# Clustered attention with two feed-forward layers: an order planned around VectorE and GpSimd, and weight pieces split on ScalarE

## Chip, cores and metric

One NeuronCore of one Trainium2 chip. The metric is the device time of one execution in microseconds (us), median of three runs. Engine names: PE is TensorE, DVE is VectorE, ACT is ScalarE, POOL is GpSimd, SP is SyncE, which issues the DMAs.

## What is computed

Two batches of eight heads, 768 positions, head size 64. A query sees only the keys that fall to the same one of 16 centroids; then come two feed-forward layers (512 to 2048 to 512), the first with SiLU, the second with PReLU:

```python
mask = q_assign[:, :, :, None] == k_assign[:, :, None, :]
scores = scale * np.matmul(q, k.transpose(0, 1, 3, 2))
scores = np.where(mask, scores, -1000000000.0)
scores = scores - np.max(scores, axis=-1, keepdims=True)
attn = np.exp(scores)
attn = attn / (np.sum(attn, axis=-1, keepdims=True) + 1e-09)
out = np.matmul(attn, v)                   # (2, 8, 768, 64) -> x: (1536, 512)
h = x @ w_in;   x = (h * (1.0 / (1.0 + np.exp(-h)))) @ w_out        # layer 1
h = x @ w2_in;  y = (np.maximum(h, 0.0) + alpha * np.minimum(h, 0.0)) @ w2_out   # layer 2
```

The inputs are float64 in HBM, so each weight matrix is 8 MB there.

## The kernel before

**Numbers.** Every matrix product is made of three fp16 products: each operand is a high half plus a low half, and high*high, high*low and low*high are added in PSUM.

**Attention.** 96 units: 12 tiles of 128 queries times 8 heads. `front` makes the scores of a unit on PE (lines 692 and 696), DVE scales them in PSUM and takes their minimum (L706), ACT makes the exponential (L711) and its high half (L718), DVE the low half (L720: fp32 value and fp16 high half in, both in SBUF). A transposing DMA (L726) turns both halves, and `back` multiplies them by V on PE (L738). K, V and Q are scaled and split first (`prep_k_*`, `prep_v*`, `prep_q_*`), largely on ACT and POOL; `pow2_scale` turns a sum of squares into a scale with a DVE step (L345) and two tiny ones, mostly on POOL (L350, L353).

**Weights.** Each of the four matrices comes in 8 pieces of 1 MB (`load_piece`, L792). `to_f32` makes fp32 of the float64 bits: two ACT operations (L803, L807) and two DVE operations with two SBUF inputs each (L814, L817). `sum_sq` takes the piece's sum of squares on PE and DVE (L848, L850), and `split` makes the fp16 halves, each 128x1024. What it costs where depends on a letter of `SPLIT`: "d" makes the high half on POOL (L824) and the low half on DVE (L825, two SBUF inputs); "a" makes the high half on ACT (L829) and the low half on DVE (L830); "b" is two ACT operations (L834, L835) and the low half on POOL (L836); "c" is POOL, ACT, POOL (L838 to L840). Before, the 32 letters hold 20 d, 8 b, 4 c and no a. Pieces of an "in" matrix are split one by one, and their raw buffer then takes the next load; pieces of an "out" matrix share one scale and are split when all eight are summed (`late`).

**Layers.** Layer 1 runs in 7 chunks of queries between the attention units: first product L1077, SiLU (L1084, L1085, L1088, L1089), second product L1108. The second layer's weights are prepared when attention is done, since they use its memory. Layer 2 has three stretches of 512 queries: `split_x2` (L1165, L1166), first product L1179 with 16 blocks, PReLU on DVE (L1188 and L1189 read PSUM), high half on ACT (L1192), low half on DVE (L1193, two SBUF inputs), then the second product L1210. Three PSUM banks take the blocks in turn.

**Order.** `Plan` takes all instructions in the order in which they were written, gives each a cost from a small table (`costs`), and places them engine by engine: each engine takes the earliest-written instruction that is ready in planned time (`run`). The result is fixed as the order in each engine's queue; waits are on data alone, and no wait is added for the plan's times.

Of the kernel before, what the change touches and what calls it, by code (L numbers as in the profile page):

```python
# [34 lines left out]

K_SCALE_ON = ("aaaa", "pppa")
V_SCALE_ON = ("papa", "appp")
SPLIT = ("dddddddd", "dddbdddb", "dbdbdbdb", "dccdcbbc")
EXP_ON = ("aaaaaaaa", "aaaaaaaa", "aaaaaaaa", "aaaaaaaa")
P_LO_DVE = range(96)  # L40

# [4 lines left out]
class Plan:  # L46
# [4 lines left out]
    def __init__(self, instructions):  # L51
        self.ins = [
            i for i in instructions
            if self.engine(i) in self.ENGINES and type(i).__name__ not in ("BassTilePoolBoundary", "InstRegisterMove")
        ]
        self.eng = [self.ENGINES.index(self.engine(i)) for i in self.ins]
        self.cost = [self.costs(i) for i in self.ins]
        self.deps = [[] for _ in self.ins]
        self.order_only = [[] for _ in self.ins]
        self.data_deps()  # L60
# [12 lines left out]
    def costs(self, i):  # L73
# [21 lines left out]
        rate = 400.0 if run >= 4096 else 290.0 if run >= 2048 else 380.0  # L95
        return (0.47, 1.3, n * 512 / 1000.0 / rate)

    def cells(self, a):
        import numpy as np

        b = a.bass_ap
        name = b.tensor.name.rsplit("_", 1)[0]
        if type(b.tensor).__name__.startswith("DRam"):
            return None, None
        it = 2 if a.dtype in (F16, BF16) else 4
        dims = [list(x) for x in a.ap]
        at = np.array([b.offset % dims[0][0]], dtype=np.int64)
        for st, c in dims[1:]:
            if st:
                at = (at[:, None] + np.arange(c) * st).ravel()  # L110
        cell = np.unique(at * it // 4)
        if name[0] in "sxmw" and (name[1:].isdigit() or len(name) == 1):
            return "ps" + name, np.unique(cell // 512)
        return name, cell

# [35 lines left out]
    def run(self, prio):  # L151
        import heapq

        N, ne = len(self.ins), len(self.ENGINES)
        after = [[] for _ in range(N)]
        left = [0] * N
        for n in range(N):
            for d in self.deps[n]:
                after[d].append((n, False))
            for d in self.order_only[n]:  # L160
                after[d].append((n, True))
            left[n] = len(self.deps[n]) + len(self.order_only[n])
        ready = [0.0] * N
        free, busy = [0.0] * ne, [-1.0] * ne
        now, later = [[] for _ in range(ne)], [[] for _ in range(ne)]
        order = [[] for _ in range(ne)]
        queue = end = 0.0
        for n in range(N):
            if not left[n]:
                heapq.heappush(later[self.eng[n]], (0.0, prio[n], n))  # L170
        for _ in range(N):
            while True:
                best = None
                for e in range(ne):
                    while later[e] and later[e][0][0] <= free[e]:
                        t, p, n = heapq.heappop(later[e])
                        heapq.heappush(now[e], (p, n))
                    t = free[e] if now[e] else later[e][0][0] if later[e] else None
                    if t is not None and (best is None or t < best[0]):
                        best = (t, e)  # L180
                t, e = best
                if now[e]:
                    break
                free[e] = t
            n = heapq.heappop(now[e])[1]
            s, c = free[e], self.cost[n]
            kind = self.ENGINES[e]
            if kind == "PE":
                if s > busy[e] + 0.02:
                    s += 0.06  # L190
                free[e] = busy[e] = s + c[0]
                done = s + c[0] + 0.23
                own = free[e]
            elif kind == "SP":
                b = max(s + c[1], queue)
                queue = b + c[2]
                free[e] = max(s + c[0] + 0.06, queue - 7.5 + c[0])
                done = own = queue + 0.33
            else:
                free[e] = s + max(c[0] - 0.075, 0.04)  # L200
                done, own = s + c[0] + 0.06, s + c[0]
            end = max(end, done)
            order[e].append(n)
            for m, only in after[n]:
                at = s if only else own if self.eng[m] == e else done
                ready[m] = max(ready[m], at)
                left[m] -= 1
                if not left[m]:
                    heapq.heappush(later[self.eng[m]], (ready[m], prio[m], m))
        return end, order  # L210
# [19 lines left out]
def cluster_attention_silu_prelu(  # L230
# [729 lines left out]
    def attention():  # L960
# [348 lines left out]
```

## Time and profile before

| what | us |
|---|---|
| median of three runs (lowest, highest) | 863.17 (862.83, 863.89) |
| profiled execution, its own time | 861.21 |
| span of its instructions | 859.3 |
| PE busy, share of the span | 726.8 (85%) |
| DVE busy | 558.5 (65%) |
| ACT busy | 437.9 (51%) |
| POOL busy | 216.8 (25%) |

The profiled execution's own time is 1.9 us over its span and 1.96 us under the median. Shares over the whole span mix stages with different limits, so the profile is read by stage. PE's clock is given as a granted share: 1.00 is its upper level of 2.4 GHz, half of it the lower level of 1.2 GHz, and a value in between is a stretch with both.

### The profile page before, as it was taken

To read this page: it belongs to the slowest core of one execution; us is meant where nothing else is said; L and a number is where in the kernel's file an instruction comes from. 1 tells how busy PE (TensorE), PEld (TensorE's weight loads), DVE (VectorE), ACT (ScalarE), POOL (GpSimd) and SP (SyncE) were. 2 spreads that over 40 slices of the span, in tenths; PEclk is the share of its full clock that TensorE was granted. 3 is DMA by queue.
4 is the path that set the end of the run, shared out by engine and by line. 5 is a ranking of instruction groups with operands and counts; after the bars stand their busy time and mean duration, and the time that the engine had idled before them with its cause. 6 is when DMAs were issued, how large, how long until landed. Compare 5 with 4: busy or idle time off the path is not lost.

```text
span 859.3 us, 16824 instructions
## 1 busy us (share of the span) xinstructions
PE 726.8 (85%) x6932; PEld 508.5 (59%) x6932; DVE 558.5 (65%) x1012; ACT 437.9 (51%) x713; POOL 216.8 (25%) x273
## 2 busy tenths in 40 slices
PE   2455557868888799999899979989989998999998
PEld 2334346657776687788777868777434443444443
DVE  5588897897868776837976876777780068106710
ACT  7835675746667756736766775865241023102210
POOL 4752412482424632200221045108200000000000
PEclk9999557789999899999999979999999999999999
DMA  9977898759999698935897984530000000000000
GB/s 281 258 189 186 184 308 138 124 104 181 139 184 163 133 175 145 153 61 100 145 146 124 280 189 154 197 147 1 1 1 19 31 1 1 12 25 13 1 24 25
DMA packets 241596, 101.89 MB, mean 119 GB/s; under 512 B 217328, under 2 KB 227568, under 8 KB 241392
## 3 DMA queue, kind: packets, MB, share of 16 engines
q1 hardware_dynamic: 241520, 100.83, 54.7%
q8 instruction: 54, 0.88, 0.4%
q14 instruction: 22, 0.18, 0.1%
HBM read 44.08 MB, written 3.15 MB: 55 GB/s over the span
## 4 chain that ended last, share of the span: by engine, by line
PE 24%; issue 16%; DVE 5%; DMA 5%; ACT 2%; POOL 2%; POOLq 0%; SPq 0%; ACTq 0%; DVEq 0%
PE w L1210 6%; PE w L1179 4%; PE w L1108 4%; PE m L1210 4%; DMA arena<-arena 2%; PE m L1179 2%; DMA arena<-in_moe_w_out_dram 2%; PE x L738 1%; DVE arena L1193 1%; DVE arena L1188 1%; PE w L1077 1%; DMA arena<-in_moe_w_in_dram 1%; DVE arena L1189 1%; PE m L1108 1%; ACT arena L1192 1%
## 5 line engine op out<-in xcount | busy, mean ns | idle before, releaser
L1108 PE MATMUL w<-arena 128*128 128x256 f16 (+1 forms) x1248 | 133.8, 260 | 9.5 <-DVE arena L825 6.4
L1108 PEld LDWEIGHTS <-arena 128*128 128x128 f16 x1344 | 117.2, 100 | 26.6 <-DVE arena L825 7.1
L1077 PE MATMUL w<-arena 128*128 128x256 f16 (+1 forms) x1200 | 130.3, 260 | 2.8 <-DVE arena L1085 2.4
L1077 PEld LDWEIGHTS <-arena 128*128 128x128 f16 x1344 | 116.8, 100 | 18.2 <-issue 4.1
L711 ACT ACTIVATE arena<-s,stat 128x768 f32<-128x768 f32 x96 | 86.1, 897 | 71.7 <-DVE s L706 39.5
L720 DVE TENSOR_TENSOR arena<-arena 128x768 f16<-128x768 f32 x96 | 99.4, 1038 | 32.0 <-ACT arena L718 31.8
L706 DVE TENSOR_SCALAR_CACHE_REDUCE s<-s,stat 128x768 f32<-128x768 f32 x96 | 97.7, 1021 | 31.8 <-PE s L696 30.1
L1179 PEld LDWEIGHTS <-arena 128*128 128x128 f16 x576 | 57.1, 99 | 76.5 <-issue 11.9
L718 ACT ACTIVATE arena<-arena 128x768 f16<-128x768 f32 x96 | 80.0, 840 | 34.2 <-DMA arena<-arena 33.8
L1210 PEld LDWEIGHTS <-arena 128*128 128x128 f16 x576 | 56.3, 98 | 68.0
L738 PE MATMUL x<-arena 128*128 128x64 f16 x1728 | 74.8, 202 | 22.7 <-DMA arena<-arena 22.1
L350 POOL TENSOR_SCALAR stat<-stat 128x1 int32<-128x1 int32 x49 | 17.7, 360 | 296.8 <-DVE stat L345 215.9
L1179 PE MATMUL w<-arena 128*128 128x512 f16 x384 | 88.0, 384 | 2.6 <-DVE arena L1189 2.5
L738 PEld LDWEIGHTS <-arena 128*128 128x128 f16 x1728 | 68.2, 104 | 33.3 <-DMA arena<-arena 29.8
L1210 PE MATMUL w<-arena 128*128 128x512 f16 x384 | 83.7, 379 | 0.0
L1192 ACT ACTIVATE arena<-arena,stat 128x512 f16<-128x512 f32 x48 | 34.5, 722 | 94.3 <-DVE arena L1189 94.3
L692 PE MATMUL s<-arena 80*128 80x384 f16 x192 | 69.0, 359 | 10.1 <-ACT arena L711 10.0
L1188 DVE TENSOR_SCALAR arena<-w,stat 128x512 f32<-128x512 f32 x32 | 23.9, 745 | 82.0 <-PE w L1179 82.0
L696 PE MATMUL s<-arena 128*128 128x384 f16 x192 | 69.5, 362 | 0.0
L1193 DVE SCALAR_TENSOR_TENSOR arena<-arena,stat 128x512 f16<-128x512 f32 x48 | 38.5, 805 | 29.5 <-ACT arena L1192 29.5
L814 DVE SCALAR_TENSOR_TENSOR arena<-arena 128x1024 int32<-128x1024 int32 x32 | 39.6, 1237 | 15.5 <-ACT arena L807 15.5
L1179 PE MATMUL m<-arena 128*128 128x512 f16 x192 | 45.4, 387 | 3.1 <-DVE arena L1189 3.0
(155 smaller groups left out, 1071.5 us busy)
## 6 DMA issues: line engine op xcount, KB each, us to landing
arena<-in_moe_w_in_dram SPq DMA_DIRECT2D x16, 1024.0 KB, 6.2
arena<-in_moe_w_out_dram SPq DMA_DIRECT2D x16, 1024.0 KB, 5.3
arena<-in_k_dram SPq DMA_DIRECT2D x8, 384.0 KB, 4.6
arena<-in_q_dram SPq DMA_DIRECT2D x6, 512.0 KB, 4.8
arena<-in_v_dram SPq DMA_DIRECT2D x8, 384.0 KB, 5.7
out_dram<-arena SPq DMA_DIRECT2D x12, 256.0 KB, 2.0
arena<-arena SPq DMA_TRANSPOSE x149, 4.1
arena<-in_moe_alpha_dram SPq DMA_DIRECT2D x1, 1024.0 KB, 5.4
```

Of the source, the lines that this page charges most:

```text
L692: nc.tensor.matmul(out=sc[:, j, :hs], lhsT=qt2[0:D + C, h], rhs=kt2[0:D + C, h % 2, j * hs:(j + 1) * hs], start=True, stop=False,)
L696: nc.tensor.matmul(out=sc[:, j, :hs], lhsT=qt1[:, h], rhs=kt1[:, h % 2, j * hs:(j + 1) * hs], start=False, stop=True,)
L706: nc.vector.tensor_scalar(sc[:, :, :hs], sc[:, :, :hs], nd_cols[:, H * (n % 2) + h:H * (n % 2) + h + 1], None, op0=ALU.mult, op1=ALU.min, ...
L711: nc.scalar.activation(out=view(o, F32, 2, hs), in_=sc[:, :, :hs], func=ACTF.Exp, scale=-1.0, bias=bias, accum_out=sums[n % 2][:, h:h + 1],)
L718: nc.scalar.activation(out=hl[:, 0], in_=p, func=ACTF.Copy)
L720: en.tensor_tensor(out=hl[:, 1], in0=p, in1=hl[:, 0], op=ALU.subtract)
L738: nc.tensor.matmul(out=x_ps[0][:, h], lhsT=pt[:, ph * T + t], rhs=vt[:, h % 2, t, vh], start=(i == 0), stop=(i == 3 * T - 1),)
L1077: nc.tensor.matmul(out=hp[:, ff], lhsT=wi[:, a, kd, ff * 128:ff * 128 + 128], rhs=mov(bb, kd), start=(i == 0), stop=(i == 3 * KD - 1),)
L1108: nc.tensor.matmul(out=acc, lhsT=wo[:, a, f % 2, dt * 128:(dt + 1) * 128], rhs=g[:, f, bb], start=(i == 0), stop=(i == 3 * KF - 1),)
L1179: nc.tensor.matmul(out=hp, lhsT=in_piece(o_a + 24 * KB, f // 2)[:, a, kd, f % 2 * 128:][:, :128], rhs=x[bb][:, kd], start=(i == 0), stop=( ...
L1193: nc.vector.scalar_tensor_tensor(out=g[:, f, 1], in0=gf, scalar=l2[:, 0:1], in1=g[:, f, 0], op0=ALU.mult, op1=ALU.subtract,)
L1210: nc.tensor.matmul(out=acc, lhsT=g[:, f, a, t * 128:(t + 1) * 128], rhs=out_piece(o_w, f // 2)[:, bb, f % 2], start=(i == 0), stop=(i == 3 ...
```

## The change

Two things. **The planner** knows a shared resource of DVE and POOL: `takes_port` is true for every POOL operation but a memset, and for DVE's tensor-tensor, scalar-tensor-tensor and copy operations whose tensor inputs all lie in SBUF. While one of the two engines is planned to run such an operation, the other passes over its own and takes the next ready one that isn't, or waits in planned time. It also charges a matmul 1.6 times its cost in planned stretches in which it holds PE's clock to be low (those lines are left out below). **The pieces**: all 32 letters of `SPLIT` become "a".

```diff
-SPLIT = ("dddddddd", "dddbdddb", "dbdbdbdb", "dccdcbbc")
+SPLIT = ("aaaaaaaa", "aaaaaaaa", "aaaaaaaa", "aaaaaaaa")
...
+    def takes_port(self, i):
+
+        e, kind = self.engine(i), type(i).__name__
+        if e == "Pool":
+            return kind != "InstMemset"
+        if e != "DVE" or kind not in ("InstTensorTensor", "InstTensorScalarPtr", "InstTensorCopy"):
+            return False
+        ins = [a for a in i.ins if hasattr(a, "bass_ap")]
+        if kind == "InstTensorScalarPtr":
+            ins = [a for a in ins if self.size(a) > 1]
+            if len(ins) < 2:
+                return False
+        return not any(self.in_psum(a) for a in ins)
...
+                held = []
+                if e in other and port[other[e]] > t:
+                    while now[e] and self.port[now[e][0][1]]:
+                        held.append(heapq.heappop(now[e]))
+                    if not now[e]:
+                        free[e] = min(port[other[e]], later[e][0][0] if later[e] else 1e9)
+                        for x in held:
+                            heapq.heappush(now[e], x)
+                        continue
+                break
...
+                if self.port[n]:
+                    port[e] = s + c[0]
```

The mode that all pieces now take is there before, unused:

```python
        elif mode == "a":
            nc.scalar.activation(out=hi, in_=t, func=ACTF.Copy, scale=s)
            nc.vector.scalar_tensor_tensor(
                out=lo, in0=t, scalar=s, in1=hi, op0=ALU.mult, op1=ALU.subtract
            )
```

Three places in the order follow. In the changed kernel lines behind the planner stand 43 further down (L711 is L754, L720 is L763, L829 and L830 are L872 and L873).

ACT around the first two exponentials of the attention, before (L553 is V's high half, L711 the exponential, L718 its high half, L803 and L807 a weight piece's conversion, L625 Q's high half):

```order
L553 ACTIVATE arena<-arena 128x12x64
L711 ACTIVATE arena,stat<-s_65,stat 128x768
L711 ACTIVATE arena,stat<-s_64,stat 128x768
L718 ACTIVATE arena<-arena 128x768 x2
L803 ACTIVATE arena<-arena 128x1024
L807 ACTIVATE arena<-arena 128x1024
```

and now, the same work as L596, L754, L761, L846 and L850:

```order
L872 ACTIVATE arena<-arena,stat 128x1024
L596 ACTIVATE arena<-arena 128x12x64
L872 ACTIVATE arena<-arena,stat 128x1024
L596 ACTIVATE arena<-arena 128x12x64
L754 ACTIVATE arena,stat<-s_65,stat 128x768
L846 ACTIVATE arena<-arena 128x1024
L761 ACTIVATE arena<-arena 128x768
L754 ACTIVATE arena,stat<-s_64,stat 128x768
```

Two high halves of weight pieces (L872) now stand in front of the first exponential.

DVE at the splitting of layer 1's "out" pieces, before (L825 a piece's low half, L720 and L706 the attention's steps):

```order
L825 SCALAR_TENSOR_TENSOR arena<-arena,stat 128x1024 x2
L720 TENSOR_TENSOR arena<-arena 128x768
L825 SCALAR_TENSOR_TENSOR arena<-arena,stat 128x1024
L720 TENSOR_TENSOR arena<-arena 128x768
L825 SCALAR_TENSOR_TENSOR arena<-arena,stat 128x1024
L706 TENSOR_SCALAR s_65,stat<-s_65,stat 128x2x384
```

and now:

```order
L749 TENSOR_SCALAR s_64,stat<-s_64,stat 128x2x384
L873 SCALAR_TENSOR_TENSOR arena<-arena,stat 128x1024 x2
L763 TENSOR_TENSOR arena<-arena 128x768
L873 SCALAR_TENSOR_TENSOR arena<-arena,stat 128x1024 x6
L763 TENSOR_TENSOR arena<-arena 128x768 x2
L803 TENSOR_TENSOR stat<-stat 128x8
L749 TENSOR_SCALAR s_65,stat<-s_65,stat 128x2x384
```

Eight low halves, where six were, now stand nearly in a row, one attention step between them.

DVE at the start of layer 2, before (L1166 is `split_x2`, L825 low halves of the last matrix, L1188, L1189 and L1193 the blocks of layer 2):

```order
L1166 SCALAR_TENSOR_TENSOR arena<-arena,stat 128x512
L825 SCALAR_TENSOR_TENSOR arena<-arena,stat 128x1024
L1166 SCALAR_TENSOR_TENSOR arena<-arena,stat 128x512 x3
L825 SCALAR_TENSOR_TENSOR arena<-arena,stat 128x1024
L1188 TENSOR_SCALAR arena<-m,stat 128x512
L1189 SCALAR_TENSOR_TENSOR arena<-m,arena 128x512
L1193 SCALAR_TENSOR_TENSOR arena<-arena,stat 128x512
```

and now (L1209, L873, L1231, L1232 and L1236):

```order
L1209 SCALAR_TENSOR_TENSOR arena<-arena,stat 128x512 x4
L873 SCALAR_TENSOR_TENSOR arena<-arena,stat 128x1024
L1231 TENSOR_SCALAR arena<-m,stat 128x512
L873 SCALAR_TENSOR_TENSOR arena<-arena,stat 128x1024
L1232 SCALAR_TENSOR_TENSOR arena<-m,arena 128x512
L873 SCALAR_TENSOR_TENSOR arena<-arena,stat 128x1024
L1236 SCALAR_TENSOR_TENSOR arena<-arena,stat 128x512
L1231 TENSOR_SCALAR arena<-w_69,stat 128x512
L873 SCALAR_TENSOR_TENSOR arena<-arena,stat 128x1024
L1232 SCALAR_TENSOR_TENSOR arena<-w_69,arena 128x512
```

Two low halves stood ahead of the first block; now eight stand among the first four blocks. In PE's order the sums that free this work (L397, now L440) stood 105 matmuls of layer 1's last product ahead of layer 2; now 21. The last sum of squares of the second weights (L848, now L891) stood 113 such matmuls ahead, now 28, and the fifteen before it stand later among PE's matmuls too.

## Rows read from the trace of the kernel before

**Rows 1.** Busy time by stretch: span, PE, PEld, DVE, ACT, POOL, PEclk, DMA, GB/s

```profile
40.00:200.00 160.00, 102.64 (x1276) 81.35 (x1277) 137.36 (x252) 93.77 (x149) 65.93 (x71) 0.81 0.81 179
200.00:480.00 280.00, 253.55 (x3398) 212.48 (x3397) 200.08 (x400) 181.67 (x328) 75.46 (x101) 0.99 0.82 144
480.00:595.00 115.00, 102.30 (x973) 88.50 (x970) 86.20 (x131) 78.98 (x109) 36.35 (x36) 0.94 0.55 163
595.00:643.00 48.00, 44.48 (x203) 20.11 (x202) 37.96 (x52) 16.58 (x26) 13.15 (x9) 0.96 0.00 1
```

**Rows 2.** PE's waits, 40 to 200 us: total, times, longest

```profile
PE w L848 <- DVE arena L817: 24.0, 11, 5.2
```

**Rows 3.** Groups of DVE, 40 to 200 us: busy us, mean ns, idle ahead

```profile
L720 DVE TENSOR_TENSOR arena<-arena 128x768 f16<-128x768 f32 x27 | 31.0, 1152 | 2.2 <-ACT arena L718 2.1
...
L825 DVE SCALAR_TENSOR_TENSOR arena<-arena,stat 128x1024 f16<-128x1024 f32 x12 | 20.4, 1705 | 1.6 <-POOL arena L824 1.5
L817 DVE SCALAR_TENSOR_TENSOR arena<-arena 128x1024 int32<-128x1024 int32 x14 | 19.7, 1412 | 0.0
```

**Rows 4.** Timeline of DVE, 76 to 186 us: start, us, operation

```profile
76.63 1.22 DVE L817 SCALAR_TENSOR_TENSOR arena<-arena 128x1024 int32<-128x1024 int32 x1
...
173.20 0.94 DVE L720 TENSOR_TENSOR arena<-arena 128x768 f16<-128x768 f32 x1
...
176.04 2.88 DVE L720 TENSOR_TENSOR arena<-arena 128x768 f16<-128x768 f32 x1
...
181.83 1.27 DVE L825 SCALAR_TENSOR_TENSOR arena<-arena,stat 128x1024 f16<-128x1024 f32 x1
183.03 2.88 DVE L720 TENSOR_TENSOR arena<-arena 128x768 f16<-128x768 f32 x1
```

**Rows 5.** Timeline of POOL at the same place, and one early row

```profile
22.67 1.11 POOL L350 TENSOR_SCALAR stat<-stat 128x1 int32<-128x1 int32 x1 [6.18 <-DVE stat L345]
23.74 0.19 POOL L353 TENSOR_SCALAR stat<-stat 128x1 int32<-128x1 int32 x1
...
175.01 3.09 POOL L836 TENSOR_TENSOR arena<-arena 128x1024 f16<-128x1024 f32 x1
```

**Rows 6.** Groups of POOL, 40 to 200 us

```profile
L824 POOL TENSOR_SCALAR arena<-arena,stat 128x1024 f16<-128x1024 f32 x12 | 19.1, 1600 | 0.0
...
L836 POOL TENSOR_TENSOR arena<-arena 128x1024 f16<-128x1024 f32 x2 | 6.3, 3126 | 0.0
```

**Rows 7.** Groups of ACT, 40 to 200 us

```profile
L711 ACT ACTIVATE arena<-s,stat 128x768 f32<-128x768 f32 x27 | 24.3, 900 | 38.4 <-DVE s L706 22.8 <-DVE arena L720 15.0 <-DVE stat L758 0.6
```

**Rows 8.** Groups of ACT over the whole span

```profile
L834 ACT ACTIVATE arena<-arena,stat 128x1024 f32<-128x1024 f32 x8 | 9.6, 1206 | 2.3 <-POOL stat L350 2.3
L835 ACT ACTIVATE arena<-arena 128x1024 f16<-128x1024 f32 x8 | 8.9, 1107 | 0.0
```

**Rows 9.** PE's waits, 480 to 595 us

```profile
PE s L848 <- DVE arena L817: 6.6, 4, 2.7
```

**Rows 10.** Timeline of PE, first product of layer 2

```profile
595.14 2.75 PE L1179 MATMUL m<-arena 128*128 128x512 f16 x12
597.73 5.34 PE L1179 MATMUL w<-arena 128*128 128x512 f16 x24
...
631.35 4.13 PE L1179 MATMUL m<-arena 128*128 128x512 f16 x12 [2.99 <-DVE arena L1189]
...
643.08 3.19 PE L1210 MATMUL w<-arena 128*128 128x512 f16 x14
```

**Rows 11.** Timeline of DVE in the same product

```profile
600.27 2.31 DVE L1193 SCALAR_TENSOR_TENSOR arena<-arena,stat 128x512 f16<-128x512 f32 x1 [0.79 <-ACT arena L1192]
602.50 0.74 DVE L1188 TENSOR_SCALAR arena<-w,stat 128x512 f32<-128x512 f32 x1
603.27 0.69 DVE L1189 SCALAR_TENSOR_TENSOR arena<-w,arena 128x512 f32<-128x512 f32 x1
...
614.63 0.75 DVE L1193 SCALAR_TENSOR_TENSOR arena<-arena,stat 128x512 f16<-128x512 f32 x1 [0.79 <-ACT arena L1192]
```

More of the change, by code (lines that the diff above doesn't have):

```diff
@@ L57, in __init__ @@
         self.cost = [self.costs(i) for i in self.ins]
+        self.port = [self.takes_port(i) for i in self.ins]
         self.deps = [[] for _ in self.ins]
@@ L96, in costs, with in_psum @@
         return (0.47, 1.3, n * 512 / 1000.0 / rate)
+    @staticmethod
+    def in_psum(a):
+        name = a.bass_ap.tensor.name.rsplit("_", 1)[0]
+        return name[0] in "sxmw" and (name[1:].isdigit() or len(name) == 1)
+    def takes_port(self, i):
[10 more added lines that the diff above has]
+        return not any(self.in_psum(a) for a in ins)
     def cells(self, a):
@@ L111, in cells @@
         cell = np.unique(at * it // 4)
-        if name[0] in "sxmw" and (name[1:].isdigit() or len(name) == 1):
+        if self.in_psum(a):
             return "ps" + name, np.unique(cell // 512)
@@ L167, in run @@
         queue = end = 0.0
+        port = [0.0] * ne
+        other = {1: 3, 3: 1}
         for n in range(N):
@@ L170, in run @@
                 heapq.heappush(later[self.eng[n]], (0.0, prio[n], n))
+        window = [0, False, 0.0]
         for _ in range(N):
@@ L181, in run @@
                 t, e = best
-                if now[e]:
-                    break
-                free[e] = t
+                if not now[e]:
+                    free[e] = t
+                    continue
[3 more added lines that the diff above has]
+                        held.append(heapq.heappop(now[e]))
+                    if not now[e]:
+                        free[e] = min(port[other[e]], later[e][0][0] if later[e] else 1e9)
+                        for x in held:
+                            heapq.heappush(now[e], x)
+                        continue
+                break
             n = heapq.heappop(now[e])[1]
+            for x in held:
+                heapq.heappush(now[e], x)
             s, c = free[e], self.cost[n]
@@ L190, in run @@
                     s += 0.06
-                free[e] = busy[e] = s + c[0]
-                done = s + c[0] + 0.23
+                w = int(s / 3.413)
+                if w > window[0]:
+                    hot = w == window[0] + 1 and window[2] > (1.36 if window[1] else 1.43)
+                    window = [w, hot, 0.0]
+                window[2] += c[0]
+                t = c[0] if window[1] else 1.6 * c[0]
+                free[e] = busy[e] = s + t
+                done = s + t + 0.23
                 own = free[e]
```

## The prediction

> **What bounds the kernel now.** I read the busy times by stretch first, since the shares of the whole span hide four different stages [rows 1]. From 40 to 200 us the reader is to see DVE at 137.4 of 160 us, PE at 102.6, ACT at 93.8: DVE sets the pace while the first weights are prepared and 28 units of attention pass. PE's waits there say the same: 24.0 us in 11 waits before the sums of squares (L848), each released by DVE's conversion L817 [rows 2]. From 200 to 480 us PE holds 253.6 of 280 us, so whatever the other engines gain counts little there, except that the whole stretch starts earlier. From 480 to 595 us, with the second weights, PE is busy 102.3 of 115 us and again waits for L817. From 595 us on PE is nearly full; in the first product of layer 2 it misses 3.5 us of 48.
>
> Then the groups of DVE in the first stretch, and their single rows. L720 has a mean of 1152 ns [rows 3], but an undisturbed one takes 0.94 us and two take 2.88 [rows 4]. The one at 176.04 ends at 178.92; POOL's L836, a low half of a weight piece, runs from 175.01 to 178.10 [rows 5]. So DVE's step, issued 1.03 us after POOL's, did its own 0.94 us only after POOL's end, less a little. The undisturbed lengths are 0.94 for L720, 1.27 for L825 and 1.22 for L817 [rows 4]. Against them the three groups hold an excess of 31.0 - 27 x 0.94 = 5.6, 20.4 - 12 x 1.27 = 5.2 and 19.7 - 14 x 1.22 = 2.6 us [rows 3], 13.4 us together. That is the prize in the stretch that DVE bounds.
>
> **The change, part by part.** *First weights (40 to 200 us).* The pieces leave POOL: L824 and L836 are 19.1 + 6.3 of its 65.9 us [rows 1, 6], 39%. Of the excess of 13.4 us, the two long L720 rows beside L836 are 2 x 1.94 = 3.9 us by name; of the other 9.5 I take POOL's 39%, so 3.7, as beside L824 and L836. That makes 7.6 us (bounds 3.9 and 13.4, since I have not matched every row to its neighbour). The other 5.8 us stand beside POOL's work for Q, K, V and x, which stays. The planner now tries to keep those apart, but its order carries no wait, and a chip that runs a microsecond off the plan meets the same collision again; I take a third, 1.9 us (0 to 5.8). Against this, the two b pieces of the "out" matrix bring DVE two more low halves, 2 x 1.27 = 2.5 us. DVE saves 7.6 + 1.9 - 2.5 = 7.0 us, and as it is busy for 86% of the stretch, I pass on 86%: **-6 us** (-11 to 0).
>
> In rows 4 and 5 DVE, which bounds the stretch, is the one that was held, 1.94 us behind a low half on POOL. The Trainium skill, page "SBUF — State Buffer", section "Summary: rules for kernel authors", says that of such a pair the second to issue blocks until the first is done, and that the one off the critical path should be the one so scheduled. The changed planner doesn't ask which is urgent, it holds whichever comes second, DVE too. By that rule the planner's third of 5.8 us would come to nothing, and the sum below to -8 in place of -10; by the rows, which show collisions of both orders, I keep the third.
>
> ACT pays. Of the 16 first pieces, 14 gave it nothing and two took two operations each; now it makes 16 high halves, 12 operations more. A's form is not in the trace; its nearest rows are L834 with a scale, 1206 ns, and L835 with an fp16 output, 1107 ns [rows 8]. I take 1.15 us: 13.8 us on an engine that is busy 93.8 of 160. I cost it at nothing: before 27 exponentials ACT stood idle for 38.4 us, waiting for DVE [rows 7]. If that cover is gone, it is the second rival below. The fifth weight load and those behind it follow their low halves on DVE as before; SP's order has the sixth load ahead of the first attention transpose, which then waits behind it in SP's queue until that piece is split. The order on ACT and DVE puts the split first as well, so I give this no cost of its own; the range holds it.
>
> *Attention and layer 1 (200 to 480 us).* No piece is split here. Only the planned order differs, and PE is at 91% [rows 1]: **-1 us** (-5 to +3), the same third of a small excess.
>
> *Second weights (480 to 595 us).* ACT keeps its count on the "in" matrix (8 high halves for 4 b pieces with two operations each), DVE gets 4 low halves more, 5.1 us, and is busy 86.2 of 115 us, so they fit. In the changed order the sums of squares stand later among PE's matmuls of layer 1, so PE comes to them when they are ready: of 12.7 us in which PE is not busy, 6.6 are waits of L848 for L817 [rows 1, 9]. I take two thirds of these: **-4 us** (-8 to 0).
>
> *Layer 2's first product (595 to 643 us).* This one gives back. A block of 12 matmuls takes 597.73 - 595.14 = 2.59 us, 16 take 41.4, and the product took 643.08 - 595.14 = 47.9 us, with one wait of 2.99 us for DVE [rows 10]. DVE needs 0.74 + 0.69 + 0.75 = 2.2 us a block [rows 11], so it has 0.4 us to spare, 6 us in all. The last matrix's eight low halves, 8 x 1.27 = 10.2 us, now stand among the first four blocks, and `split_x2` with 3 us of DVE ahead of them can start only 21 matmuls before the product does. The excess over the spare, 10.2 + 3 - 6, is 7 us of PE's waits; before it was 6.5 us over the ideal, part of it from L1193 rows as long as 2.31 us beside POOL's pieces, which now are gone [rows 11]. **+1 us** (-2 to +6).
>
> The rest of layer 2 has no piece and the same order on DVE. Sum: -6 - 1 - 4 + 1 = -10 us against the profiled execution's own 861.2, so 851; that execution is 2 us under the median of the runs shown, so the median is **853 us**. PE's total of matmuls does not change, and PE is what ends the kernel, so a gain in the first stretch moves all that follows. The case's own range, with the terms' bounds taken as independent, is 846 to 860.
>
> **The rivals.**
>
> *Gain and more (0.12).* The granted clock is 0.81 from 40 to 200 us [rows 1]: some 38% of it at 1.2 GHz. If the shorter waits also bring PE to 2.4 GHz for half of that, 0.19 x 160 us at 64% PE busy is 19 us of PE time, and half of it, 10 us, comes off: 843. Against it: PE is not the bound there.
>
> *ACT takes DVE's place (0.14), the other side.* The place is the head of the attention, where two high halves now stand before the first exponential and more before the next ones. The chain of a unit is L706 on DVE, L711 and L718 on ACT, L720 on DVE. If that chain, and not DVE's sum of work, sets the pace, each high half ahead of a ready exponential delays a unit by 1.15 us: 16 x 1.15 = 18 us, less what DVE saves, 7.0, is +11 in place of -6; with the other terms' -4 that gives 870. It decides from the point where the high halves exceed ACT's wait before L711, 38.4 us over 27 [rows 7]; 18 is under it, which speaks against. For it: these waits are uneven, and ACT's queue is in a fixed order.
>
> *Nothing is left (0.10): POOL is held instead.* DVE's added low halves are themselves two-input steps, and POOL still makes every scale. L350 took 1.11 us at 22.67, and the like step L353 behind it 0.19 [rows 5]. If each of the 12 low halves more holds up one such step ahead of ACT's high half, 12 x 0.92 = 11 us come back: 864. It is also the result if the planned times drift so far that nothing is kept apart. The same section of the Trainium skill makes no difference between the two engines as to who is held; the L350 row, made while DVE was converting a piece, agrees. Against: POOL's wait is mostly on DVE's results, and a late scale costs only if its piece is late.
>
> **How the numbers follow.** The forecast has 0.64, the larger gain 0.12, ACT 0.14, nothing left 0.10. Range 841 to 863: it leaves out the slower rival and a little below. About 0.2% is what a measurement of this kernel can tell from no change: 861.4 to 864.9. Faster 0.76, same 0.10, slower 0.14.
>
> **What would show it.** L720, L825's successor L830 and L817 near 0.94, 1.27 and 1.22 us in the first 200 us, DVE's busy time in 40 to 200 us some 7 us smaller, and layer 2 starting some 11 us earlier than 595: then the first step is right. Two-input steps of 2 us or more beside POOL's K, V and Q work show that the planner's part does nothing. PE waits of some 7 us in layer 2's first product show the give-back. The prediction is wrong if ACT's idle time before the exponential is gone while PE waits for it, or if the first stretch is no shorter though the collisions are gone: then the chain, not DVE's work, was the bound.

## The result and the profile after

The changed kernel takes 830.6 us (829.0 to 831.9) beside 863.0 us for the kernel before: ratio 0.9633, 95% interval 0.9595 to 0.9671. That is 32 us less; I had forecast 10 less, with a range from 841 to 863. The profiled execution's own time is 829.6 us, its span 827.8.

The busy times by stretch of the kernel after, as in [rows 1]; the second row ends where the first row of [rows 1] ends in work, at the exponential of unit 28 (199.19 us before, 178.27 now), the fourth and the fifth likewise end with layer 1 and with layer 2's first product. Units and chunks are counted from 0, pieces and loads from the first. Columns: stretch, length, busy us of PE, PEld, DVE, ACT and POOL, granted clock, DMA share, GB/s.

```profile
40.00:200.00 160.00, 119.63 (x1582) 96.38 (x1583) 143.89 (x287) 118.11 (x188) 43.47 (x61) 0.88 0.91 199
40.00:179.00 139.00, 100.53 (x1240) 79.62 (x1241) 127.05 (x249) 102.24 (x154) 39.17 (x54) 0.86 0.92 208
200.00:480.00 280.00, 255.60 (x3290) 214.03 (x3287) 198.42 (x393) 179.85 (x319) 68.13 (x97) 0.98 0.83 148
480.00:568.50 88.50, 82.15 (x769) 72.62 (x770) 62.80 (x106) 57.76 (x78) 6.03 (x20) 0.96 0.51 164
568.50:613.60 45.10, 42.94 (x204) 19.86 (x202) 41.97 (x60) 22.43 (x31) 0.34 (x2) 1.00 0.00 1
```

For the same work up to unit 28, DVE was busy 137.36 of 160 us before and is busy 127.05 of 139 now. Its busy time fell by 10.3 us, **and its idle time from 22.6 to 12.0 us**. The second half of this is what I did not forecast. (Counted from the span's start in place of 40 us, the two fell by 11.8 and 9.1 us.) DVE's waits over the two stretches (what waited, for what: total, times, longest), the first two lines before, the third after:

```profile
DVE s L706 <- PE s L696: 5.9, 8, 1.8
DVE has L593 <- PE m L589: 3.5, 3, 1.5
DVE s L749 <- PE s L739: 1.7, 3, 0.7
```

The wait for a unit's scores fell from 5.9 to 1.7 us, and that for a small product of PE (L589), 3.5 us, is no longer there. These two make 7.7 of the 10.7 us.

PE's waits from 40 to 180 us of the kernel after, the answer to [rows 2], and below them the wait of L735 as it was from 40 to 200 us of the kernel before (L692); the groups of DVE there, the answer to [rows 3] (busy us, mean ns | idle ahead); and two groups of ACT, the answer to [rows 7, 8]:

```profile
PE w L891 <- DVE arena L860: 16.4, 7, 8.5
PE s L735 <- ACT arena L754: 10.4, 6, 4.1
PE s L692 <- ACT arena L711: 7.9, 7, 3.8
```

```profile
L763 DVE TENSOR_TENSOR arena<-arena 128x768 f16<-128x768 f32 x28 | 27.2, 984 | 3.0 <-ACT arena L761 3.0
L873 DVE SCALAR_TENSOR_TENSOR arena<-arena,stat 128x1024 f16<-128x1024 f32 x14 | 18.7, 1373 | 0.0
L860 DVE SCALAR_TENSOR_TENSOR arena<-arena 128x1024 int32<-128x1024 int32 x14 | 17.1, 1218 | 0.0
```

```profile
L754 ACT ACTIVATE arena<-s,stat 128x768 f32<-128x768 f32 x27 | 24.1, 894 | 7.6 <-DVE s L749 4.4 <-DVE arena L763 2.5 <-DVE stat L390 0.3
L872 ACT ACTIVATE arena<-arena,stat 128x1024 f16<-128x1024 f32 x14 | 15.9, 1174 | 5.6 <-POOL stat L393 5.6
```

The two-input steps are near their undisturbed lengths: L763 has a mean of 984 ns where its predecessor L720 had 1152, L860 1218 where L817 had 1412. ACT's idle time ahead of the exponential fell from 38.4 to 7.6 us.

Where the time went, by the start of the same instruction in both timelines (the n-th of its line in program order):

| up to | before | after | gained so far | in this part | forecast |
|---|---|---|---|---|---|
| exponential, unit 28 | 199.2 | 178.3 | 20.9 | 20.9 | 6 (0 to 11) |
| first conversion of the second weights | 480.3 | 462.7 | 17.6 | -3.3 | 1 (-3 to 5) |
| layer 1's last matmul | 595.0 | 568.5 | 26.5 | 8.9 | 4 (0 to 8) |
| layer 2's first product done | 643.1 | 613.6 | 29.5 | 3.0 | -1 (-6 to 2), all of layer 2 |
| layer 2's last stretch, DVE's first step of it | 775.0 | 743.6 | 31.5 | 2.0 | |

### The profile page after: what moved, and what is told of

Its sections match the earlier page's. It is cut to its first block, busy times and chain, and to the rows that moved or that the text cites. A ratio compares the mean times of both kernels' runs of the same rounds, so it can differ in the third digit from the quotient of the medians.

```text
span 827.8 us, 16776 instructions
## 1 busy us (share of the span) xinstructions
PE 722.4 (87%) x6932; PEld 508.4 (61%) x6932; DVE 544.7 (66%) x1024; ACT 450.4 (54%) x725; POOL 140.9 (17%) x237
## 5 line engine op out<-in xcount | busy, mean ns | idle before, releaser
L763 DVE TENSOR_TENSOR arena<-arena 128x768 f16<-128x768 f32 x96 | 92.3, 966 | 29.3 <-ACT arena L761 28.7
L754 ACT ACTIVATE arena<-s,stat 128x768 f32<-128x768 f32 x96 | 85.9, 895 | 40.5 <-DVE arena L763 19.3
L781 PE MATMUL x<-arena 128*128 128x64 f16 x1728 | 75.2, 202 | 26.6 <-DMA arena<-arena 26.5
L761 ACT ACTIVATE arena<-arena 128x768 f16<-128x768 f32 x96 | 80.3, 839 | 30.9 <-DMA arena<-arena 30.2
L1222 PE MATMUL w<-arena 128*128 128x512 f16 x384 | 86.1, 379 | 3.3 <-DVE arena L1232 3.3
L1253 PE MATMUL w<-arena 128*128 128x512 f16 x384 | 83.7, 379 | 0.0
L735 PE MATMUL s<-arena 80*128 80x384 f16 x192 | 70.5, 367 | 14.6 <-ACT arena L754 10.7
L1231 DVE TENSOR_SCALAR arena<-w,stat 128x512 f32<-128x512 f32 x32 | 23.8, 745 | 78.2 <-PE w L1222 78.2
L1236 DVE SCALAR_TENSOR_TENSOR arena<-arena,stat 128x512 f16<-128x512 f32 x48 | 35.8, 750 | 24.7 <-ACT arena L1235 24.2
L857 DVE SCALAR_TENSOR_TENSOR arena<-arena 128x1024 int32<-128x1024 int32 x32 | 40.2, 1258 | 14.7 <-ACT arena L850 14.6
L846 ACT ACTIVATE arena<-arena 128x1024 int32<-128x1024 uint32 x32 | 36.7, 1147 | 23.3 <-DMA arena<-in_moe_w_out_dram 17.6
```

What stands on the lines that cost most here:

```text
L735: nc.tensor.matmul(out=sc[:, j, :hs], lhsT=qt2[0:D + C, h], rhs=kt2[0:D + C, h % 2, j * hs:(j + 1) * hs], start=True, stop=False,)
L754: nc.scalar.activation(out=view(o, F32, 2, hs), in_=sc[:, :, :hs], func=ACTF.Exp, scale=-1.0, bias=bias, accum_out=sums[n % 2][:, h:h + 1],)
L761: nc.scalar.activation(out=hl[:, 0], in_=p, func=ACTF.Copy)
L763: en.tensor_tensor(out=hl[:, 1], in0=p, in1=hl[:, 0], op=ALU.subtract)
L781: nc.tensor.matmul(out=x_ps[0][:, h], lhsT=pt[:, ph * T + t], rhs=vt[:, h % 2, t, vh], start=(i == 0), stop=(i == 3 * T - 1),)
L857: nc.vector.scalar_tensor_tensor(out=lo, in0=hi, scalar=3, in1=lo, op0=ALU.logical_shift_left, op1=ALU.bitwise_or)
```

## Experiments

Two more measures serve here. The *excess* of a kernel is the time by which DVE's steps are longer than the lower quartile of their own line and shape (counted from 0.1 us up): 39.1 us before, 14.4 after; from 40 us to unit 28 it is 14.7 and 5.1. And for each kernel I read DVE's busy and idle time from 40 us up to unit 28's exponential:

| kernel | ratio to before (95%) | unit 28 | DVE busy | DVE idle | excess to unit 28 |
|---|---|---|---|---|---|
| before | 1 | 199 | 137.4 | 22.6 | 14.7 |
| after | 0.9633 (0.9595 to 0.9671) | 178 | 127.1 | 12.0 | 5.1 |
| e1, planner alone | 1.0152 (1.0122 to 1.0182) | 202 | 131.1 | 31.9 | 10.4 |
| e2, letters alone | 0.9828 (0.9804 to 0.9853) | 190 | 131.7 | 19.3 | 6.9 |
| e3, no hold | 0.9711 (0.9679 to 0.9743) | 185 | 130.0 | 16.0 | 6.0 |
| e4, no clock charge | 0.9570 (0.9528 to 0.9612) | 182 | 124.4 | 18.6 | 1.8 |
| f1, after with late loads | 0.9780 (0.9751 to 0.9810) | 193 | 127.0 | 27.0 | 5.1 |
| f2, before with early loads | 1.0002 (0.9987 to 1.0017) | 200 | 137.7 | 23.3 | 14.3 |
| h1, letters, pieces first | 0.9842 (0.9806 to 0.9878) | 187 | 129.1 | 18.9 | 4.2 |
| h2, before with pieces first | 0.9814 (0.9755 to 0.9874) | 189 | 136.1 | 13.9 | 13.5 |

The ratio is from several executions, the other columns from the profiled one alone, and that need not lie at the median: e4's took 828.2 us (median 822.4), f1's 844.7 (841.5), h2's 839.2 (843.9). i2, the same kernel as e4 with a profiled execution of 822.1 us, has unit 28 at 178.0 and 14.5 us of DVE's idle time, so some 4 us in these columns are scatter.

### The two parts, and the parts of the planner

e1 is the changed planner with the old letters, e2 the old planner with the new ones:

```diff
-SPLIT = ("aaaaaaaa", "aaaaaaaa", "aaaaaaaa", "aaaaaaaa")
+SPLIT = ("dddddddd", "dddbdddb", "dbdbdbdb", "dccdcbbc")
```

> The changed planner (hold and clock charge) with the old 32 letters. Theory 1, the letters: a weight piece's chain is shorter when its high half doesn't queue on GpSimd, its raw buffer comes free earlier and the next load starts earlier; the planner's order adds the collisions of Q, K and V. Then this kernel gains only some 8 to 12 us of the 32, about 853 us, and the sixth weight load is issued near 58 us as before. Theory 2, the planner: the order that keeps the two engines apart carries most of it, whoever makes the high half; then about 840 us, and the two-input steps of VectorE are near their undisturbed lengths.

Measured: 873.7 us, **slower than before**. Neither theory had that.

> The old planner with all letters a. Theory 1, the letters: most of the gain, about 840 us (-23), the sixth weight load issued near 42 us in place of 58, and collisions left only beside the Q, K and V work. Theory 2, the planner: about 855 us (-8), since VectorE still meets GpSimd's Q, K and V work. If the two parts only work together (ScalarE's added work needs the new order), both this and the planner alone stay above 850.

Measured: 845.6 us, somewhat less than theory 1 had. The two parts gain 32 us together where they give +13 and -15 apart. What the planner costs with the old letters shows in e1's POOL timeline (start, length, line, operation, shapes, count):

```profile
173.03 2.82 POOL L879 TENSOR_TENSOR arena<-arena 128x1024 f16<-128x1024 f32 x1
175.83 3.34 POOL L867 TENSOR_SCALAR arena<-arena,stat 128x1024 f16<-128x1024 f32 x2
179.14 3.08 POOL L879 TENSOR_TENSOR arena<-arena 128x1024 f16<-128x1024 f32 x1
184.64 3.59 POOL L667 TENSOR_SCALAR arena<-arena,stat 128x512 f32<-128x512 f32 x1
```

and in its waits of ACT and of PE from 165 to 192 us:

```profile
ACT arena L668 <- POOL arena L667: 13.8, 1, 13.8
```

```profile
PE s L735 <- ACT arena L754: 17.2, 1, 17.2
```

Q's scale (L667) stands behind the last matrix pieces in POOL's queue; ACT waits 13.8 us for it and PE 17.2 us for the exponential behind that. This is the smaller part of the loss: e1's profiled execution is 2.8 us behind the kernel before at unit 28, 4.6 at layer 1's last matmul and 16.1 at the end of layer 2's first product, which takes 59.4 us in place of 47.9 (g2 below shows the like of it).

e3 takes out the hold, e4 the charge of 1.6:

```diff
-                if e in other and port[other[e]] > t:
+                if False and e in other and port[other[e]] > t:
```

```diff
-                t = c[0] if window[1] else 1.6 * c[0]
+                t = c[0]
```

> The changed kernel without the hold: the planner doesn't pass over a step because the other engine is on the shared resource, and keeps its charge for a slow matmul clock. Theory 1, the letters: 834 to 838 us, only the Q, K and V collisions come back, 4 to 7 us in the first 200 us. Theory 2, the planner's hold: 845 us or more, and the excess of VectorE's two-input steps, 14 us in the changed kernel, goes back to 25 or more.

Measured: 835.7 us, excess 19.9 us (14.4 with the hold): in theory 1's range.

> The changed kernel without the charge of 1.6 for matmuls in slow planned stretches; the hold stays. Theory 1, the letters: 831 us within 2. Rival, the charge: it is what moves the sums of squares of the second weights back among the matmuls of layer 1, and so the 10 us of 480 to 595 us; then about 840 us, with the time from the first to the second product of chunk 5 back near 43 us from 32.5.

Measured: 822.4 us, faster than either expected, and chunk 5 went from its first to its second product in 34.3 us: the charge isn't what gains there. Chunk 5's 43.3 us became 32.5 after, 34.1 in e1 and 34.3 in e4, but 42.1 in e2 and 43.1 in e3. So that gain belongs to the hold (36.7 and 38.7 with one engine held, f3 and f4 below). The changed kernel as it is (i1) and the same without the charge (i2, e4's edit) stood side by side once more:

> The changed kernel as it is, beside the next one on the same chip: ratio 0.963 to 0.966 to the kernel before, 829 to 832 us.

> The changed kernel without the clock charge, the fastest so far. If the charge's order is worse once the hold is there: ratio 0.953 to 0.959, 5 us or more under the kernel beside it. If the two differ by one execution's scatter only: within 3 us of it.

Measured: 0.9641 (0.9606 to 0.9675) and 0.9567 (0.9535 to 0.9600), 828.7 and 822.6 us. The kernel without the charge is the faster one, by more than their intervals. Their timelines part at unit 64: from there to unit 72 it is 50.7 us with the charge (50.6 in the kernel before) and 42.0 without. Between units 32 and 64 both lose 4 to 5 us of what they had gained. e3, without the hold, doesn't: from unit 32 to 64 it takes 135.5 us, before 139.2, after 145.0, e1 146.7.

### Two loads in SyncE's queue

SP's issues in the kernel before, and in the kernel after (start, time until issued, line; L792 and L835 are weight loads, L726 and L769 attention transposes, L629 and L672 Q's):

```profile
43.77 1.41 SPq L726 DMA_TRANSPOSE arena<-arena  x1
51.18 1.23 SPq L629 DMA_TRANSPOSE arena<-arena  x1
57.77 1.65 SPq L792 DMA_DIRECT2D arena<-in_moe_w_in_dram  x2
```

```profile
36.69 3.20 SPq L835 DMA_DIRECT2D arena<-in_moe_w_in_dram  x2
40.36 6.58 SPq L769 DMA_TRANSPOSE arena<-arena  x2
```

The sixth load is the first of the pair at 57.77, and now the second of the pair at 36.69. f1 puts it and the eighth back, f2 puts them forward in the kernel before, in the planned order of SP alone:

```diff
+    for a, side, b in moves:
+        for line in order:
+            if place[a] in line:
+                line.remove(place[a])
+                line.insert(line.index(place[b]) + side, place[a])
...
-    plan_order(tc, nc, starts)
+    plan_order(tc, nc, starts, [(loads[5], 0, loads[6]), (loads[7], 1, turns[3])])    # f1
+    plan_order(tc, nc, starts, [(loads[5], 0, turns[0]), (loads[7], 1, loads[6])])    # f2
```

> The changed kernel with two weight loads put back in SyncE's queue alone: the sixth load stands behind the transposes of the first two attention units again, as it did before, and the eighth behind those of the third and fourth. All else is as in the changed kernel. Theory 3, the queue: what the first stretch gained beyond the collisions comes from these two loads being issued earlier; then the conversion of the sixth piece goes from 57 back to about 70 us, unit 28's exponential from 178 to about 186, and the time to about 839 us. Rival, VectorE's and ScalarE's order carry it and the loads are hidden: 831 us within 2, with unit 28's exponential where it was.

Measured: 841.5 us, ratio 0.9780 in place of 0.9633. The row of f1 up to unit 28:

```profile
40.00:194.00 154.00, 103.56 (x1226) 81.50 (x1227) 127.02 (x247) 102.21 (x155) 36.30 (x54) 0.94 0.83 186
```

DVE's busy time is that of the kernel after to 0.1 us, the excess too; its idle time is 27.0 in place of 12.0 us. Where it comes from (in f1, L853 and L857 are a piece's conversion on ACT, L879 its high half, L880 its low half, L864 its conversion on DVE):

```profile
ACT arena L853 <- DMA arena<-in_moe_w_in_dram: 16.5, 2, 10.2
DVE arena L880 <- ACT arena L879: 8.5, 1, 8.5
DVE arena L864 <- ACT arena L857: 5.6, 1, 5.6
```

ACT waits twice for a load, 10.2 us for the sixth and 6.3 for the eighth. Behind the first wait stands in ACT's queue the high half that DVE needs (8.5 us), behind the second the piece's own conversion (5.6 us); the sixth piece is converted on DVE at 65.2 us in place of 56.6. Up to unit 28 the kernel after has none of the three waits. This is the cleanest pair of all: 15 us at unit 28 without a collision more or less. At the end the two profiled executions are 15.1 us apart too, the medians 11, since f1's was its slowest.

> The kernel before, old letters and old planner, with the same two loads put forward in SyncE's queue: the sixth ahead of the first attention transpose, the eighth directly behind the seventh. Nothing else moves. Theory 3, the queue: the sixth piece is converted near 62 in place of 75 us and the time falls by some 6 to 10 us, to about 853. Rival, the loads are hidden or the transposes that now stand behind them pay it back: 861 us within 2.

Measured: 861.1 us, ratio 1.0002. The load, the second of this pair, was issued 20 us earlier:

```profile
34.84 2.23 SPq L797 DMA_DIRECT2D arena<-in_moe_w_in_dram  x2
```

but the sixth piece was converted at 75.8 us, as before at 75.4. On DVE's order its conversion stands behind the scores of six units before, of two units after. So the early load is needed where ACT's and DVE's orders ask for the piece early, and worth nothing where they don't. Nor is it the only way to gain: in e3 the sixth load is issued at 50.1 us and the sixth piece converted at 70.5, and unit 28 comes 13.8 us earlier than before.

### Which engine is held

Both are e4 with one entry left out:

```diff
-        other = {1: 3, 3: 1}
+        other = {3: 1}    # f3: GpSimd alone is held
+        other = {1: 3}    # f4: VectorE alone is held
```

> Letters a and the planner's hold without the clock charge (822 us with the hold on both engines, 846 without any), here with GpSimd alone passing over its steps while VectorE is on the shared resource; VectorE is never held. If the hold is worth something because VectorE, which bounds the first stretch, isn't disturbed (that is how the Trainium skill, page SBUF - State Buffer, section Summary: rules for kernel authors, reads), this is as good as the hold on both, 820 to 825 us. Rival: the gain is that of another order on VectorE, which this kernel doesn't get; then 835 to 845.

> The same with VectorE alone passing over its steps while GpSimd is on the shared resource; GpSimd is never held. If holding the engine that bounds the stretch costs what it gives, 840 to 848 us. Rival, the gain is that of the other order on VectorE: 822 to 828 us, with the sixth load ahead of the first transposes as with the hold on both.

Measured: f3 829.9 us (0.9645, 0.9616 to 0.9674), f4 834.2 us (0.9692, 0.9657 to 0.9727), where both held give 822 and none 846. Each alone gains, and both lie between their two forecasts, so neither theory is borne out. f3 lies nearer the better number, but the intervals overlap. The Trainium skill, page "SBUF — State Buffer", section "Summary: rules for kernel authors", has as its rule that the one to be scheduled is the one off the critical path; these two runs neither show nor refute it. That holding the critical engine too still gains, 830 to 822, the rule doesn't tell.

In the excess of the whole span: none held 19.0 us, GpSimd 16.4, VectorE 14.4, both 10.7.

### The old letters, one matrix at a time

```diff
-SPLIT = ("aaaaaaaa", "aaaaaaaa", "aaaaaaaa", "aaaaaaaa")
+SPLIT = ("aaaaaaaa", "dddbdddb", "aaaaaaaa", "aaaaaaaa")    # g1
+SPLIT = ("aaaaaaaa", "aaaaaaaa", "aaaaaaaa", "dccdcbbc")    # g2
+SPLIT = ("dddddddd", "aaaaaaaa", "dbdbdbdb", "aaaaaaaa")    # g3
```

> The changed kernel with the old letters for layer 1's out matrix alone (six d, two b). The planner with all old letters took 874 us; its trace has two places where POOL's queue holds up others. If the first, POOL splitting pieces ahead of Q's scale near 168 to 188 us with ScalarE and PE waiting 14 to 17 us behind it, comes from this matrix, the time is 843 to 850 us, unit 28's exponential near 194 in place of 178. Rival, the loss comes from the first matrix and the order ahead of it: 831 us within 3.

Measured: 839.0 us (0.9761, 0.9730 to 0.9792); unit 28 at 186.6, up to unit 20 nothing changed. The place is right; unit 28 lost half of what I had named, and the time lies 4 us under my range.

> The changed kernel with the old letters for layer 2's out matrix alone (c, d and b mixed). My forecast had the change lose 1 us in layer 2's first product since eight low halves come to VectorE; the measured layer 2 gained 5 to 6. If the pieces on POOL were what disturbed that product, this kernel loses 6 to 12 us, all of it behind 568 us: 837 to 843 us. Rival, the gain there comes from elsewhere (order of the sums of squares): 831 us within 2.

Measured: 843.8 us (0.9810, 0.9780 to 0.9840), nothing lost up to layer 1's last matmul (568.3 against 568.5). That is the forecast of the first theory and a little more. POOL in g2 (L881 a piece's fp32 copy, L879 and L883 low halves), and the waits behind it:

```profile
571.73 5.00 POOL L883 TENSOR_TENSOR arena<-arena 128x1024 f16<-128x1024 f32 x2
578.23 3.08 POOL L879 TENSOR_TENSOR arena<-arena 128x1024 f16<-128x1024 f32 x1
581.28 3.10 POOL L883 TENSOR_TENSOR arena<-arena 128x1024 f16<-128x1024 f32 x1
```

```profile
ACT arena L882 <- POOL arena L881: 10.9, 2, 8.2
DVE arena L1209 <- ACT arena L1208: 6.9, 1, 6.9
PE m L1222 <- DVE arena L1232: 7.7, 1, 7.7
```

ACT stands 8.2 us before L882, whose input POOL makes late; behind it in ACT's queue is `split_x2` (L1208), for which DVE waits 6.9 us, and PE 7.7 us for DVE.

> The changed kernel with the old letters for the two in matrices alone (eight d; four d, four b). The planned order then has the sixth weight load behind two attention transposes again. If that matrix's split on ScalarE is what lets the order be the one that gains 12 us up to unit 8, the time is 838 to 843 us, with unit 8's exponential near 95 in place of 88.7. Rival, the out matrices carry it: 831 to 834 us.

Measured: 839.3 us (0.9762, 0.9731 to 0.9793), unit 8 at 92.2, the sixth conversion at 61.8 in place of 56.6. The three losses, as ratios 0.0128, 0.0177 and 0.0129, make 0.043 of the 0.052 between after and e1: they nearly add.

### Orders without the hold

g4 is e4 with this:

```diff
-K_SCALE_ON = ("aaaa", "pppa")
-V_SCALE_ON = ("papa", "appp")
+K_SCALE_ON = ("aaaa", "aaaa")
+V_SCALE_ON = ("aaaa", "aaaa")
```

> Letters a, the hold, no clock charge (822 us), and the scales of K and V that GpSimd still made (seven of sixteen) on ScalarE. Of the 10.7 us by which VectorE's steps there are still longer than undisturbed, 4.2 stand beside these scales. If collisions are what a microsecond of the time is made of: 818 to 820 us. Rival, the time follows the order: its planned order has the sixth load behind the first two transposes again, and then 828 to 836 us though there are fewer collisions.

Measured: 836.5 us (0.9718, 0.9682 to 0.9753), 14 us slower than e4. The excess did not fall (11.5 against 10.7 us; other pairs met), so this says nothing on the price of a collision; it shows how far a small edit shifts the whole order.

h1 to h4 have the planner take the first matrix's pieces earlier, by a fixed number of instructions; `early` puts the names of what a piece issues into `ahead`. h1 and h3 (100 in place of 200) are e2 with this edit, h2 is the kernel before with it, h4 is e4 with it:

```diff
-    end, order = plan.run(list(range(len(plan.ins))))
+    end, order = plan.run([n - 200 * (i.name in ahead) for n, i in enumerate(plan.ins)])
...
+        conv, scale = early(conv), early(scale)
```

> Letters a and the old planner (846 us), with one edit: the planner takes the conversion and splitting of the first matrix's pieces as if they had been written 200 instructions earlier. Its order has the sixth piece converted behind two units' scores on VectorE (before six, changed kernel two) and the sixth load ahead of the first transpose. Theory 4, the order of pieces and units sets the first stretch: 832 to 837 us, the sixth conversion near 57 us, VectorE busy for over 92% of 40 to 180 us though nothing keeps the engines apart. Rival, the hold's gain is the undisturbed VectorE: 846 us within 3.

Measured: 846.8 us, no gain over e2. The sixth piece came earlier (converted at 62.5 us, e2 69.8), but unit 4 later (77.5 against 73.1). My theory 4, that earlier pieces are the gain, fell here.

> The kernel before with the same edit of 200 instructions: old letters, no hold. If the order alone is enough: 846 to 852 us, a gain of 10 to 15 us up to unit 28. If the order needs the high halves on ScalarE, because POOL's queue makes each piece wait: 857 to 866 us, with the sixth conversion no earlier than 70 us.

Measured: 843.9 us (0.9814, 0.9755 to 0.9874), with all old letters on POOL and no hold. Its row up to unit 28:

```profile
40.00:190.00 150.00, 101.75 (x1315) 82.01 (x1315) 136.13 (x254) 92.92 (x150) 65.27 (x70) 0.76 0.85 188
```

The excess is that of before (39.9 us in all), the time 16 us less. DVE's idle time from 40 us to unit 28 fell from 22.6 to 13.9 us; this kernel does 4.7 us less of DVE's work ahead of 40 us, though, and counted from the span's start DVE's idle time fell by 3.8 us and its busy time by 6.3. The profiled execution is h2's fastest, its span 21.9 us shorter than that of the one before: 10.1 of that were gained up to unit 28, 10.5 between units 64 and 72, far behind the pieces that were moved.

> As the first of these four, by 100 instructions in place of 200. Its order has the sixth load behind two transposes and the sixth conversion behind four units. Theory 4: between, 839 to 845 us. Rival: 846 us within 3, as the other dose.

> Letters a, the hold without the clock charge (822 us, the fastest so far), and the 200 instructions on top: pieces and loads still earlier than in any kernel here, the twelfth load behind four transposes. If earlier pieces are always better: 815 to 820 us. If the first units of attention are now what comes late (unit 4 behind more pieces), 824 to 835 us.

Measured: h3 842.1 us (0.9790, 0.9756 to 0.9824), in the range foreseen, but the intervals of h3 and h1 both overlap that of e2, so neither dose is shown to gain; h4 832.0 us (0.9668), slower than e4: its unit 4 starts at 86.0 us (e4 71.9).

## Why the prediction was wrong

All four terms came out beyond their bounds, the first by most.

**First weights: -6 forecast, -20.9 measured.** The collisions were sized right. I had 7.6 us from pieces leaving POOL and 1.9 from the planner, 9.5 together; from 40 us to unit 28 the excess fell from 14.7 to 5.1, by 9.6 us, of which 7.8 are there with the letters alone (e2). DVE's busy time fell by 10.3 where I had 7.0. DVE waited for none of ACT's twelve more high halves (no idle time ahead of L873), 1174 ns each.

The step that failed is "as it is busy for 86% of the stretch, I pass on 86%". It takes DVE's idle time as a constant share. The changed order halved that idle time, by 10.7 us, as much as DVE's work gave. With it failed the sentence on the sixth load: "I give this no cost of its own; the range holds it". In f1 that load and the eighth cost 15 us at unit 28 and 11 at the end. Shown is that this idle time follows the order of the queues (f1, the same work on DVE); which change in the order took away which part of the 10.7 us is not shown.

**Attention and layer 1: -1 forecast, +3.3 measured**, a little outside its bounds. The loss lies between units 32 and 64. It is there with and without the clock charge, and on the same letters and charge it goes with the hold: 145.0 us with it, 135.5 without (e3). Why the held order is slower there stays open; h4, held too, takes 138.9. The charge is a part of the diff that my sum did not cost at all: without it 8.7 us more are gained between units 64 and 72, and 6 at the end.

**Second weights: -4 (-8 to 0) forecast, -8.9 measured.** The mechanism was the one named, sums of squares later among PE's matmuls, but it is the smaller part. The last of these sums stands 28 matmuls ahead of layer 2 in after, e1 and e4, which have the hold; it stands 113 ahead before, 169 and 173 in e2 and e3. From chunk 5's first product to layer 1's last matmul PE waits for L817 ahead of these sums 6.6 us before, 3.8 after, 13.3 in e2 and 9.4 in e3. So 2.8 us of the gain are in the wait that I had named. The two windows of chunk 5 from its first to its second product, before and after:

```profile
467.50:510.80 43.30, 36.19 (x390) 30.44 (x388) 32.84 (x58) 29.75 (x46) 12.46 (x13) 0.88 0.93 216
```

```profile
448.90:481.40 32.50, 29.90 (x355) 25.88 (x353) 27.76 (x46) 26.09 (x44) 2.76 (x4) 0.99 0.98 236
```

PE's time not busy, for whatever reason, fell from 7.1 to 2.6 us; the other 6.3 us are 35 matmuls that moved behind (2.9 us of that came back by the end of layer 1) and the granted clock, 0.99 in place of 0.88.

**Layer 2: +1 forecast, -5.0 measured.** PE in the first product after, and some of its blocks:

```profile
568.62 2.75 PE L1222 MATMUL m<-arena 128*128 128x512 f16 x12
582.19 2.75 PE L1222 MATMUL w<-arena 128*128 128x512 f16 x12 [0.36 <-DVE arena L1232]
586.50 2.75 PE L1222 MATMUL m<-arena 128*128 128x512 f16 x12 [0.78 <-DVE arena L1232]
590.27 5.34 PE L1222 MATMUL w<-arena 128*128 128x512 f16 x24 [1.02 <-DVE arena L1232]
613.58 2.75 PE L1253 MATMUL w<-arena 128*128 128x512 f16 x12
```

The product takes 45.0 us (47.9 before), with 2.2 us of waits where I had 7. DVE's eight low halves are there, and DVE is busy 42.0 of 45.1 us. e2 and e3, with letters a and no hold, have them ahead of the product, and it takes 43.8 us: the give-back that I had looked for is 1.1 us. What I left out of the excess over the spare is PE's lead: three banks let it run three blocks ahead, 3 x 2.59 = 7.8 us, which by this working covers the 7 [rows 10]; no run tests that by itself. That the old pieces on POOL cost more in this place, g2 shows: 14.8 us in this product. The last 2 us, in the second stretch, lie in one block of PE and the wait for DVE ahead of it, before and after:

```profile
718.76 4.44 PE L1179 MATMUL w<-arena 128*128 128x512 f16 x12 [2.19 <-DVE arena L1189]
688.97 2.75 PE L1222 MATMUL w<-arena 128*128 128x512 f16 x12 [1.90 <-DVE arena L1232]
```

The wait is 0.3 us shorter, and the block behind it 1.7, since the granted clock in that block was 0.61 before, most of it at 1.2 GHz, and 1.00 after, 2.4 GHz. In the first product the block behind the wait of 2.99 us [rows 10] likewise took 4.13 in place of 2.75 us, at 0.66.

**The rivals.** The time came out beyond "gain and more", but its mechanism doesn't carry it: up to unit 28 the granted clock was 0.81 before and 0.86 after, but 0.81 in i1, the changed kernel once more, which reached unit 28 at 177.0 us. e3 gained 13.8 us up to there at 0.75. ACT did not take DVE's place, though half of the sign that I had named for it appeared: ACT's idle time ahead of the exponential fell from 38.4 to 7.6 us, and PE's waits for the exponential rose from 7.9 to 10.4. DVE is busy 127.1 of the 139 us, ACT 102.2, and the stretch got shorter. "Nothing left" is right in one respect: with the old letters (e1) the hold does make POOL's queue hold up others.

**What is shown and what is not.** Shown: on the same letters, orders alone move the time by up to 23 us (e2 to e4); an order alone with every collision left gains 16 (h2); in the changed kernel's order the early loads are necessary to what the first stretch gained (f1), and in the order before they are not sufficient (f2). Not shown: a rule for which order is good; earlier pieces (h1, h4) is not that rule. Nor is there a price of a collision: from e2 to e4, without the charge, the hold takes 8.3 us off the excess and 23 off the time, but from e3 to the changed kernel, with the charge, 5.5 off the excess and some 5 to 7 off the time.

## To carry to other kernels

Where the bounding engine is idle for a seventh of its stretch, ask what it waits for before passing a saving on in proportion: a new order can remove the idle time too, and here that was as much again. When a planner's costs change, cost the order of every queue, the DMA queue first, and compare where each load stands against the work that shares its queue; then ask whether its consumer's order wants it early. Change one of two interacting parts alone before believing the sum: here one was worth +13 alone and -17 on top of the other's -15.

## What I had not expected of the hardware

The granted clock did not follow the time: up to unit 28 it was 0.94 in f1 (193 us), 0.86 in the changed kernel (178 us), 0.75 in e3 (185 us) and 0.81 before (199 us). Executions of one program scatter by up to 1.4% (839.2 to 851.0 us for h2; 818.2 to 825.7 for i2), so a difference of 0.7% between two orders can't be read from single executions. A low half of a weight piece took 1278 ns on average with POOL idle (eight in layer 2's first product), against 1373 in the first stretch beside POOL's work.
